# Attention, then two feed-forward layers, on one core: VectorE's next unit waits for GpSimd, and rows of the fixed cycle move

## The chip, the cores and the metric

One NeuronCore of a Trainium2 chip runs the whole program. The metric is device time in microseconds (us) of one execution, the median over repeated runs. Engines are named as the profile names them: PE is TensorE's matmuls and PEld its weight loads, DVE is VectorE, ACT ScalarE, POOL GpSimd, SP SyncE (which here only issues DMAs).

## The reference

```python
scores = (q @ k.T) / sqrt(64)                  # 4 batches x 8 heads, 576 x 576, head size 64
kth    = 32nd largest score of each row
attn   = softmax(scores kept where >= kth)
x = attn @ v                                   # as 2304 tokens x 512
h = x @ w_in;   P = a0 + a1*h + a2*h^2 + a3*h^3      # layer 1, 512 -> 2048 -> 512
Q = 1 + |b0|*|h| + |b1|*h^2;   x = (P / (Q + 1e-6)) @ w_out
h = x @ w2_in;  out = (h * cos(h)) @ w2_out    # layer 2, 512 -> 2048 -> 512
```

Everything is float32. To keep that precision with PE's faster float32 form, each operand is split into a high and a low part, and three products (high x high, low x high, high x low) are summed.

## The kernel before

**Units and groups.** Attention runs in 72 units. A unit is 128 queries by one pair of heads; eight units (4 head pairs by 2 halves) make a block of 256 tokens. In the last eight units, 64 to 71, a unit's queries come from two batches. Each feed-forward layer treats a block in eight groups of 256 hidden columns. The pieces of a unit are generators: `qk` (scores into the PSUM tile `sx`, copied by ACT to `sS`, one copy for each head), `topk` (VectorE folds the scores into pairwise maxima and minima in `e`, two TENSOR_TENSOR rows, finds the 32 largest by MAX8 and MATCH_REPLACE8, then ACT writes the exponentials into `e`, and VectorE masks them by two SCALAR_TENSOR_TENSOR rows), `av` (PE transposes `e` into `pp..a`, `pp..b` and a part of `sx`, ACT copies these to `pt..`, PE multiplies by `v`), and `norm`.

**Layer 1** (line 498 on): `in1` and `in1b` are the two halves of h (24 matmuls); `copy1` makes w = h and r = |w| on ACT, `lin1` q = b1*r + b0 and u = -(a3*w + a2) on ACT, `pol1` q *= r and u *= w on GpSimd, `rec1` 1/Q by Ln and Exp on ACT, `mid1` and `end1` finish the quotient on VectorE and copy its high part to a tile `gg` on ACT, `low1` makes the low part on GpSimd, and `out1` (24 matmuls into `y`) multiplies by w_out. **Layer 2**: `in2`, `in2b`, `copy2` (h to `hs`), `phase2` and `mid2` (argument of the cosine, `rr` and `n`), `sin2` (on every second group, a table load and one Sin for two groups), `mul2`, `high2`, `low2`, and `out2` (12 matmuls of 512 columns into `o`).

**The order.** Early units are placed by a scheduler. From unit U0 = 20 to unit U1 = 72 the order is written out by hand in `unit(i, prev)` (line 843): the wrapper `InOrder` (line 90) chains each engine's instructions in the order in which they are written. A unit works at once on its own maxima, on the masks, transposes and values of unit i-1, on the scores of unit i+2, on layer 1 of group i-9 and i-10, and on layer 2 of groups i-18 to i-21. In a *sine* unit (every second one, the even ones) ACT also computes the Sin.

**VectorE against GpSimd.** `InOrder` makes each GpSimd instruction wait (a semaphore) for the latest VectorE instruction, in written order, that is not a `max` or `match_replace` (`V.shared`, lines 105 to 108). GpSimd's work of a unit thus stands beside VectorE's maxima. Nothing makes VectorE wait for GpSimd at the start of the next unit, other than data.

**Buffers.** `ps_t` has two PSUM buffers, shared in turn by the two transposes, layer 1's h, `norm` and layer 2's h. `gg` has three. Weights' low parts and `w2o` stream through four 512 KB buffers on SP's queue. After unit 71 the functions `free` and `events` order the rest of the feed-forward work.

Of the kernel before, what the change touches and what calls it, by code (L numbers as in the profile page):

```python
# [89 lines left out]
class InOrder(Windowed):  # L90
    def __init__(self, *a, behind=None):
        super().__init__(*a)
        self.last = self.shared = None
        self.behind = behind

    def __getattr__(self, name):
        f = super().__getattr__(name)

        def call(*a, **k):
            r = f(*a, **k)  # L100
            if C0 <= self.piece < C1:
                if self.last is not None:
                    self.tc.add_manual_dep(r.ins, self.last, ORDER, reason="order")
                self.last = r.ins.name
                if self.behind is not None and self.behind.shared is not None:
                    self.tc.add_manual_dep(r.ins, self.behind.shared, WAIT, reason="port")
                if name not in ("max", "match_replace"):
                    self.shared = r.ins.name
            else:
                self.shared = None  # L110
# [5 lines left out]
def body(tc, out, qt, kt, vt, ident_d, w1_d, w1o_d, a_d, b_d, w2_d, w2o_d):  # L116
# [5 lines left out]
    with ExitStack() as ctx:  # L122
# [39 lines left out]
        def store_k(x, b, pr):  # L162
            raw, hi = x[:, 0].bitcast(F32), x[:, 1]
            A.activation(hi, raw, AF.Copy)
            G.tensor_sub(raw, raw, hi.bitcast(F32))
# [3 lines left out]
            for o, i_ in ((d[top, 0], hi[top]), (d[bot, 0], raw[top]), (d[bot, 1], hi[bot]), (d[top, 1], raw[bot])):  # L169
                SP.dma_start(out=o, in_=i_)  # L170

# [332 lines left out]
        def copy1(k, g):  # L504
            h, _ = g1[k, g]
            w, q, r, u = (mo.tile([P, BT * 2], F32, tag="m1" + t, bufs=NU if t == "u" else N1, name=f"{t}{k}_{g}") for t in "wqru")
            A.activation(w, h, AF.Copy)
            A.activation(r, w, AF.Abs)
            g1[k, g] = (q, r, u, w)

        def lin1(k, g):
            q, r, u, w = g1[k, g]
            A.activation(q, r, AF.Identity, scale=b1, bias=b0)
            A.activation(u, w, AF.Identity, scale=na3, bias=na2)

        def pol1(k, g):
            q, r, u, w = g1[k, g]
            E1 = V if k >= DV1 else G
            E1.tensor_mul(q, q, r)
            E1.tensor_mul(u, u, w)  # L520
# [109 lines left out]
        def out2(k, g):  # L630
# [7 lines left out]
            for i, t in steps if g < NG - 1 else sorted(steps, key=lambda x: x[1]):  # L638
                f, ts = 2 * g + i, slice(t * P, (t + 1) * P)
                for l, r in ((gh, 0), (gh, 1), (gl, 0)):  # L640
                    PE.matmul(o[:, t, :], l[:, i, ts], wt[i][:, r], start=(f == 0 and r == 0 and l is gh), stop=(f == NF - 1 and l is gl), skip_group_check=True)
# [92 lines left out]
        nrm, low, held, x2, ob = [], [], [], [], []  # L734
# [74 lines left out]
        def early(u, p):  # L809
            if p == 0:  # L810
                ev(u - UA - 1, mid1)
            if p == 1:
                lows()
                ev(u - UA, in1, in1b, copy1, lin1, pol1, rec1)
# [11 lines left out]
        def events(u, p):  # L826
# [3 lines left out]
            if p == 1:  # L830
# [4 lines left out]
                ev(u - UA, in1, in1b, copy1, lin1, pol1, rec1)  # L835
# [7 lines left out]
        def unit(i, prev):  # L843
            sine = (i - UB - 1) % SINB == SINB - 1
            t = topk(i)
            next(t)
# [3 lines left out]
            next(a)  # L850
            if not sine:
                ev(i - UB - 1, phase2)
            ev(i - UA - 1, mid1, end1)
# [7 lines left out]
            ev(i - UB - 1, mid2)  # L861
            for k in x2:
                x2low(k)
            x2.clear()
            ev(i - UB - 3, low2)
# [9 lines left out]
            if i % 4 == 0:  # L875
                next(nrm[-1])
            high_q(i + 3, True)
            ev(i - UA, in1b, copy1)
# [3 lines left out]
            ev(i - UA, lin1, pol1)  # L882
            ev(i - UB, in2)
            next(nq, None)
            ev(i - UB, in2b)
            for k in ob:
                store(k, 1)
            ob.clear()
            if i + 3 < nu:
# [3 lines left out]
            ev(i - UB - 1, table)  # L893
            for _ in range(4):
                next(t)
            load_v(i)
# [6 lines left out]
            ev(i - UB, copy2)  # L903
            ev(i - UB - 2, high2)
            if not sine or i == U1 - 1:
# [6 lines left out]
            for x, a in held:  # L912
                store_k(x, *a)
            held[:] = [(prep(*a), a) for a in preps.get(i, [])]
# [8 lines left out]
        for u in range(UB + NB * NG + 3):  # L923
            grouped = U0 <= u < U1
            f = free(u, prev) if not grouped and u <= nu else iter(())
            for p in range(5):
# [9 lines left out]
                else:  # L936
                    prev = next(f, prev)
# [42 lines left out]
```

## Time and profile before

| | us |
|---|---|
| median of 3 runs | 1382.33 (1380.45 to 1382.46) |
| the profiled execution, device time | 1381.68 |
| its span, first to last instruction | 1379.7 |
| fixed cycle, roughly 355 to 1190 of the span | 835 |

The profiled execution is a typical run: 0.65 us under the median. Its span is 1.98 us shorter than its device time, so a change of the span is taken as the same change of the time. A row of a list by line gives operation, output<-inputs, shape, count, busy us and mean ns, then the idle time just before these instructions and what ended it. A row of a timeline gives start and duration in us; the bracket is idle time before it and its releaser. Matmuls overlap in the pipe, so their spacing, start to start, is what one costs.

### The profile page before, as it was taken

What the parts mean: (1) busy time and instruction counts of PE and PEld (TensorE: products, weight loads), DVE (VectorE), ACT (ScalarE), POOL (GpSimd) and SP (SyncE); (2) the same over time, 40 slices, a digit from 0 to 9 for tenths busy, and PEclk for the clock granted to TensorE, in tenths of its full rate; (3) what the DMA queues carried; (4) which work ended last, traced back from release to release, by engine and by line L of the source; (5) the groups of instructions that cost most, each with busy time, mean ns of one, the idle gap of its engine ahead of it and who ended that gap; (6) DMA issues with size and microseconds to landing.
All of it is one profiled execution on the core that took longest, in us unless ns stands there. A gap on an engine that the chain in (4) does not pass through costs nothing.

```text
span 1379.7 us, 25048 instructions
## 1 busy us (share of the span) xinstructions
PE 1238.5 (90%) x8944; PEld 1095.0 (79%) x8944; DVE 1183.7 (86%) x2514; ACT 1086.5 (79%) x1869; POOL 585.2 (42%) x483
## 2 busy tenths in 40 slices
PE   7766777666999999999999999999999999999987
PEld 3434555556899898899988998988999899999976
DVE  6999878989999999999999899999999888655532
ACT  7887788775878888888888888888887777877642
POOL 2667545543345544444544454444444343520000
PEclk9677799777999999999999999999999999999999
DMA  8986787873456677666677766666576777677677
GB/s 263 326 279 215 240 244 233 296 256 104 136 188 207 228 238 247 223 197 221 205 230 234 254 207 208 215 219 216 189 238 239 255 264 248 212 229 245 219 236 231
DMA packets 155948, 314.98 MB, mean 228 GB/s; under 512 B 12592, under 2 KB 47536, under 8 KB 155824
## 3 DMA queue, kind: packets, MB, share of 16 engines
q1 hardware_dynamic: 122832, 261.99, 57.5%
q10 hardware_dynamic: 32992, 51.39, 11.6%
q8 instruction: 71, 1.16, 0.3%
q14 instruction: 53, 0.43, 0.1%
HBM read 278.20 MB, written 35.13 MB: 227 GB/s over the span
## 4 chain that ended last, share of the span: by engine, by line
PE 48%; ACT 15%; DVE 14%; DMA 8%; issue 2%; POOL 1%; ACTq 0%; SPq 0%; DVEq 0%; POOLq 0%
PE h L80 18%; PE o L80 11%; PE y L80 10%; PE sx L80 7%; DVE e L80 6%; DVE hd L80 5%; ACT r L80 2%; ACT sS L80 2%; DMA lo<-w1lo 2%; DMA w2o<-w2o 2%; ACT n L80 1%; ACT rr L80 1%; ACT e L80 1%; DVE rr L80 1%; DVE cb L80 1%
## 5 line engine op out<-in xcount | busy, mean ns | idle before, releaser
L80 DVE MAX8 hd<-e 128x8 f32<-128x288 f32 (+1 forms) x576 | 321.2, 597 | 0.0
L80 DVE MATCH_REPLACE8 e<-hd,e 128x288 f32<-128x288 f32 (+1 forms) x432 | 231.2, 542 | 0.0
L80 PE MATMUL y<-gg,w1o 128*128 128x256 f32 x1152 | 217.4, 287 | 7.1 <-POOL gg L80 4.2
L80 POOL TENSOR_TENSOR gg<-rr,gg 128x512 fp32r<-128x512 f32 x56 | 72.8, 1300 | 352.9 <-DVE rr L80 309.6
L80 PE MATMUL o<-w2o,gg 128*128 128x512 f32 x864 | 212.3, 393 | 3.8 <-DMA w2o<-w2o 3.8
L80 PEld LDWEIGHTS y<-gg,w1o 128*128 128x128 f32 x1152 | 183.4, 195 | 9.1 <-POOL gg L80 5.3
L80 PE MATMUL h<-xh,w1hi 128*128 128x256 f32 x576 | 178.6, 310 | 10.3 <-ACT pt41a L80 1.0
L80 PEld LDWEIGHTS o<-w2o,gg 128*128 128x128 f32 x864 | 157.6, 189 | 34.8 <-DMA w2o<-w2o 5.2
L80 PE MATMUL h<-xh,lo 128*128 128x256 f32 x576 | 166.7, 289 | 2.0 <-DMA lo<-w1lo 2.0
L80 PE MATMUL h<-xl,w1hi 128*128 128x256 f32 x576 | 167.3, 291 | 0.0
L80 PE MATMUL h<-x2h,lo 128*128 128x256 f32 x576 | 163.9, 285 | 2.3 <-DMA lo<-w2lo 2.3
L80 PE MATMUL y<-gg,w1ol 128*128 128x256 f32 x576 | 164.6, 286 | 0.0
L80 PE MATMUL h<-x2h,w2hi 128*128 128x256 f32 x576 | 163.5, 284 | 0.5 <-ACT hs L80 0.5
L80 PE MATMUL h<-x2l,w2hi 128*128 128x256 f32 x576 | 163.6, 284 | 0.1
L80 DVE TENSOR_TENSOR e<-sS 128x576 f32<-128x576 f32 x144 | 151.0, 1085 | 6.9 <-ACT sS L80 5.3
L80 PEld LDWEIGHTS h<-xh,w1hi 128*128 128x128 f32 x576 | 114.1, 198 | 29.5 <-issue 5.7
L80 DVE SCALAR_TENSOR_TENSOR e<-sS,hd,e 128x576 f32<-128x576 f32 x144 | 124.2, 889 | 14.2 <-ACT e L80 14.2
L80 POOL TENSOR_TENSOR cb<-cb,raw 128x512 int32<-128x512 int32 x64 | 89.3, 1400 | 103.1 <-DVE cb L80 85.0
L80 ACT ACTIVATE e<-sS,nb 128x576 f32<-128x576 f32 x144 | 105.6, 771 | 22.4 <-DVE hd L80 21.4
L80 PE MATMUL sx<-k,q 128*128 128x288 f32 (+1 forms) x576 | 108.2, 316 | 12.2 <-ACT sS L80 4.9
L80 PEld LDWEIGHTS h<-xh,lo 128*128 128x128 f32 x576 | 113.7, 197 | 2.6 <-DMA lo<-w1lo 2.6
L80 PEld LDWEIGHTS h<-xl,w1hi 128*128 128x128 f32 x576 | 114.1, 198 | 1.5 <-issue 0.5
(1024 smaller groups left out, 3255.8 us busy)
## 6 DMA issues: line engine op xcount, KB each, us to landing
w2o<-w2o SPq DMA_DIRECT2D x144, 512.0 KB, 4.4
lo<-w1lo SPq DMA_DIRECT2D x72, 512.0 KB, 4.2
w1ol<-w1ol SPq DMA_DIRECT2D x72, 512.0 KB, 4.8
lo<-w2lo SPq DMA_DIRECT2D x72, 512.0 KB, 4.1
k<-kdr ACTq DMA_DIRECT2D x44, 576.0 KB, 4.2
raw<-w SPq DMA_DIRECT2D x32, 512.0 KB, 5.1
v<-vt ACTq DMA_DIRECT2D x48, 320.0 KB, 4.4
qr<-qt ACTq DMA_DIRECT2D x72, 128.0 KB, 3.4
```

The lines of the kernel that those rows point to most:

```text
L80: r = f(*a, **k)
```

## The change

1. `V.ahead = G.last`: from unit 21 on, the first VectorE instruction of a unit (the first of the two TENSOR_TENSOR rows into `e`) waits for the last GpSimd instruction of the unit before.
2. In units that are not sine units, `mid2` moves behind the first maxima (max, replace, max) and is *quiet*: GpSimd doesn't wait for it.
3. `copy1` takes over `lin1` and writes w, u, r, q; `pol1` multiplies u by w first, then q by r.
4. The second head's scores stand behind all 24 matmuls of layer 2's input, no longer between its halves; their copy to `sS` stands behind the exponentials on ACT.
5. `out2` issues six matmuls, and the other six (`out2b`) behind the next transposes.
6. Phases move: `phase2`, `high2`, `copy2`, the splitting of k for the later batches (`split_k`) and one step of `norm` stand elsewhere in the unit, most of them split between sine and other units.

```diff
@@ InOrder.__getattr__
+                if self.ahead is not None:
+                    self.tc.add_manual_dep(r.ins, self.ahead, WAIT, reason="port")
+                    self.ahead = None
-                if name not in ("max", "match_replace"):
+                if name not in ("max", "match_replace") and not self.quiet:
                     self.shared = r.ins.name
@@ copy1, lin1, pol1
             A.activation(w, h, AF.Copy)
+            A.activation(u, w, AF.Identity, scale=na3, bias=na2)
             A.activation(r, w, AF.Abs)
+            A.activation(q, r, AF.Identity, scale=b1, bias=b0)
...
+            E1.tensor_mul(u, u, w)
             E1.tensor_mul(q, q, r)
-            E1.tensor_mul(u, u, w)
@@ out2
+            part(steps[:2])
+            if U0 <= PE.piece // 5 < U1:
+                rest2.append((part, steps[2:]))
+            else:
+                part(steps[2:])
@@ unit
+            if i > U0:
+                V.ahead = G.last
             next(t)
             next(prev)
             next(prev)
             a = av(i - 1)
             next(a)
+            out2b()
+            ev(i - UA - 1, mid1, end1)
             if not sine:
+                ev(i - UB - 3, high2)
                 ev(i - UB - 1, phase2)
-            ev(i - UA - 1, mid1, end1)
+                for x, a_ in held:
+                    split.append(split_k(x, *a_))
+                    next(split[-1])
+                held.clear()
...
-            ev(i - UB - 1, mid2)
             for k in x2:
                 x2low(k)
             x2.clear()
+            if not sine:
+                next(t)
+                V.quiet = True
+            ev(i - UB - 1, mid2)
+            V.quiet = False
...
-            if i % 4 == 0:
+            if i % 8 == 0 or i % 8 == 5:
                 next(nrm[-1])
+            for x in split:
+                next(x, None)
+            split.clear()
             high_q(i + 3, True)
-            ev(i - UA, in1b, copy1)
+            ev(i - UA, in1b, copy1, pol1)
             load_q(i + 4)
             nq = qk(i + 2) if i + 2 < nu else iter(())
             next(nq, None)
-            ev(i - UA, lin1, pol1)
-            ev(i - UB, in2)
-            next(nq, None)
-            ev(i - UB, in2b)
+            ev(i - UB, in2, in2b)
...
+            ev(i - UB - 1, table)
+            if not sine:
+                ev(i - UB, copy2)
+                ev(i - UB - 2, high2)
+            for _ in range(4 if sine else 3):
+                next(t)
+            next(nq, None)
+            load_v(i)
...
             ev(i - UA - 1, out1)
             ev(i - UB - 3, out2)
-            ev(i - UB - 1, table)
-            for _ in range(4):
-                next(t)
-            load_v(i)
+            if sine:
+                ev(i - UB, copy2)
             ev(i - UA, rec1)
...
-            ev(i - UB, copy2)
-            ev(i - UB - 2, high2)
-            if not sine or i == U1 - 1:
+            if not sine:
                 ev(i - UB, phase2)
...
-            for x, a in held:
-                store_k(x, *a)
-            held[:] = [(prep(*a), a) for a in preps.get(i, [])]
+            held.extend((prep(*x), x) for x in preps.get(i, []))
```

Three places as the instructions stand in the program. First TensorE between units 40 and 42: `o2` is layer 2's output, `pp41` the transposes of unit 41, `h0_4_1` layer 1's input. Before:

```order
L80 MATMUL o2_6769<-w2o2_8_7453,gg2_4_7408 128x512 x6
L80 MATMUL o2_6769<-w2o2_9_7455,gg2_4_7408 128x512 x6
L80 MATMUL pp41a_7630<-ident_98,e41_7412 128x128 x4
L80 MATMUL pp41b_7637<-ident_98,e41_7412 128x128 x4
L80 MATMUL sx_91<-ident_98,e41_7412 128x128
L80 MATMUL h0_4_1_7664<-xh4_7402,w1hi_116 128x256
```

Of the change:

```order
L80 MATMUL o2_6790<-w2o2_8_7460,gg2_4_7441 128x512 x6
L80 MATMUL pp41a_7624<-ident_98,e41_7404 128x128 x4
L80 MATMUL pp41b_7631<-ident_98,e41_7404 128x128 x4
L80 MATMUL sx_91<-ident_98,e41_7404 128x128
L80 MATMUL o2_6790<-w2o2_9_7462,gg2_4_7441 128x512 x6
L80 MATMUL h0_4_1_7664<-xh4_7398,w1hi_116 128x256
```

Six matmuls went from ahead of the transposes to behind them. Second, ScalarE in unit 41, from the copy of layer 1's h on (`w4_0` to `q4_0`), with the two score copies `sS43` and the exponentials `e41`. Before:

```order
L80 ACTIVATE w4_0_7495<-h0_4_0_7457 128x512
L80 ACTIVATE r4_0_7497<-w4_0_7495 128x512
L80 DMA qr45_7501<-qt 128x2x128
L80 ACTIVATE sS43_7503<-sx_91 128x576
L80 ACTIVATE q4_0_7496<-r4_0_7497,babs_105 128x512
L80 ACTIVATE u4_0_7498<-w4_0_7495,nega_107 128x512
L80 ACTIVATE sS43_7503<-sx_91 128x576
L80 DMA k44_2_7545<-kdr_90 128x1152
L80 ACTIVATE nb_41_7414<-hd_41_7413 128x2
L80 ACTIVATE e41_7412<-sS41_7089,nb_41_7414 128x576 x2
```

Of the change:

```order
L80 ACTIVATE w4_0_7507<-h0_4_0_7464 128x512
L80 ACTIVATE u4_0_7510<-w4_0_7507,nega_107 128x512
L80 ACTIVATE r4_0_7509<-w4_0_7507 128x512
L80 ACTIVATE q4_0_7508<-r4_0_7509,babs_105 128x512
L80 DMA qr45_7517<-qt 128x2x128
L80 ACTIVATE sS43_7519<-sx_91 128x576
L80 ACTIVATE hs2_7_7552<-h1_2_7_7527 128x512
L80 ACTIVATE gg2_5_7554<-rr2_4_7031 128x512
L80 ACTIVATE nb_41_7406<-hd_41_7405 128x2
L80 ACTIVATE e41_7404<-sS41_7099,nb_41_7406 128x576 x2
L80 ACTIVATE sS43_7519<-sx_91 128x576
L80 DMA k44_2_7572<-kdr_90 128x1152
```

The first score copy now stands behind u, r and q, the second behind the exponentials. Third, VectorE in unit 41 around the row of the phase (`rr2_6`), and at the start of unit 42, with the semaphores that each row waits for. Before:

```order
L80 TENSOR_TENSOR q43_7276<-qr43_7087,q43_7276 128x256 [waits DMAHW4_49]
L80 SCALAR_TENSOR_TENSOR rr2_6_7437<-n2_6_7438,rr2_6_7437 128x512 [waits Activation_49]
L80 MAX hd_41_7413<-e41_7412 128x8 x2
...
L80 TENSOR_TENSOR e42_7623<-sS42_7298 128x2x288 [waits PE_49]
L80 TENSOR_TENSOR e42_7623<-sS42_7298 128x2x288
```

Of the change:

```order
L80 TENSOR_TENSOR q43_7276<-qr43_7097,q43_7276 128x256 [waits DMAHW4_49]
L80 MAX hd_41_7405<-e41_7404 128x8 x2
L80 MATCH_REPLACE e41_7404<-hd_41_7405,e41_7404 128x288 [waits DVE_49] x2
L80 MAX hd_41_7405<-e41_7404 128x8 [waits DVE_49] x2
L80 SCALAR_TENSOR_TENSOR rr2_6_7443<-n2_6_7444,rr2_6_7443 128x512 [waits Activation_49]
...
L80 TENSOR_TENSOR e42_7617<-sS42_7302 128x2x288 [waits PE_49,Pool_49]
L80 TENSOR_TENSOR e42_7617<-sS42_7302 128x2x288
```

The phase's row went behind six rows of maxima, and the first row of unit 42 has a wait for GpSimd more.

## Rows read from the trace of the kernel before

**Rows 1.** Page: busy us, share of the span and instructions of each engine.

```profile
PE 1238.5 (90%) x8944; PEld 1095.0 (79%) x8944; DVE 1183.7 (86%) x2514; ACT 1086.5 (79%) x1869; POOL 585.2 (42%) x483
```

**Rows 2.** One stretch, the cycle: length, busy of PE, PEld, DVE, ACT, POOL, granted clock, DMA.

```profile
355.00:1190.00 835.00, 815.31 (x6435) 749.12 (x6435) 771.38 (x1711) 700.95 (x1187) 388.01 (x331) 1.00 0.67 222
```

**Rows 3.** List by line, PEld alone, 355 to 1190 us; idle time is the last part.

```profile
L80 PEld LDWEIGHTS h<-xh,w1hi 128*128 128x128 f32 x416 | 78.8, 190 | 27.7 <-issue 5.7 <-ACT pt41a L80 1.2 <-ACT pt25a L80 1.2
L80 PEld LDWEIGHTS sx<-k,q 128*128 128x128 f32 x472 | 65.7, 182 | 14.8 <-ACT sS L80 14.3
```

**Rows 4.** Waits of PEld, 355 to 1190 us: total us, times, longest.

```profile
PEld h L80 <- issue: 5.7, 33, 0.2
PEld h L80 <- DMA lo<-w1lo: 2.6, 3, 1.0
```

**Rows 5.** Timeline of PEld: transposes of units 22, 41, 42, 63, unit 41's two waits.

```profile
392.37 0.59 PEld L80 LDWEIGHTS pp21a<-ident,e 128*128 128x128 f32 x4
...
692.97 0.59 PEld L80 LDWEIGHTS pp40a<-ident,e 128*128 128x128 f32 x4
...
694.48 0.19 PEld L80 LDWEIGHTS h<-xh,w1hi 128*128 128x128 f32 x1 [0.38 <-ACT pt40a L80]
...
701.25 0.56 PEld L80 LDWEIGHTS sx<-k,q 128*128 128x128 f32 x4 [0.34 <-ACT sS L80]
...
708.71 0.58 PEld L80 LDWEIGHTS pp41a<-ident,e 128*128 128x128 f32 x4
...
1041.55 0.58 PEld L80 LDWEIGHTS pp62a<-ident,e 128*128 128x128 f32 x4
```

**Rows 6.** Timeline of PE in unit 41: output 2, transposes, scores, both halves of input 2.

```profile
690.44 2.92 PE L80 MATMUL o<-w2o,gg 128*128 128x512 f32 x12
693.20 0.60 PE L80 MATMUL pp40a<-ident,e 128*128 128x128 f32 x4
...
698.98 0.70 PE L80 MATMUL sx<-k,q 128*128 128x288 f32 x4
699.52 0.28 PE L80 MATMUL h<-x2h,w2hi 128*128 128x256 f32 x1
...
701.88 0.28 PE L80 MATMUL h<-x2h,w2hi 128*128 128x256 f32 x1
```

**Rows 7.** Timeline of ACT, units 40 and 41, from h's copy on.

```profile
684.17 0.63 ACT L80 ACTIVATE r<-w 128x512 f32<-128x512 f32 x1
684.79 0.65 ACT L80 ACTIVATE sS<-sx 128x576 f32<-128x576 f32 x1
685.34 0.81 ACT L80 ACTIVATE q<-r,babs 128x512 f32<-128x512 f32 x1
686.04 0.80 ACT L80 ACTIVATE u<-w,nega 128x512 f32<-128x512 f32 x1
...
687.40 1.28 ACT L80 ACT_TABLE_LOAD   x1
...
688.93 0.78 ACT L80 ACTIVATE e<-sS,nb 128x576 f32<-128x576 f32 x1
...
699.24 0.60 ACT L80 ACTIVATE w<-h 128x512 f32<-128x512 f32 x1 [1.41 <-PE h L80]
```

**Rows 8.** Timeline of POOL at the end of unit 40.

```profile
686.22 1.30 POOL L80 TENSOR_TENSOR q<-q,r 128x512 f32<-128x512 f32 x1 [0.74 <-ACT q L80]
687.48 1.81 POOL L80 TENSOR_TENSOR u<-u,w 128x512 f32<-128x512 f32 x1
```

**Rows 9.** Timeline of DVE, units 40 to 42.

```profile
672.69 1.41 DVE L80 TENSOR_TENSOR e<-sS 128x576 f32<-128x576 f32 x2
...
686.62 3.28 DVE L80 TENSOR_TENSOR e<-sS 128x576 f32<-128x576 f32 x2
...
690.56 0.81 DVE L80 SCALAR_TENSOR_TENSOR e<-sS,hd,e 128x576 f32<-128x576 f32 x1
...
696.48 0.69 DVE L80 SCALAR_TENSOR_TENSOR rr<-n,rr 128x512 f32<-128x512 f32 x1 [0.91 <-ACT n L80]
```

More of the change, by code (lines that the diff above doesn't have):

```diff
@@ L92, in __init__ @@
         super().__init__(*a)
-        self.last = self.shared = None
+        self.last = self.shared = self.ahead = None
+        self.quiet = False
         self.behind = behind
@@ L160, in load_k0, with split_k @@
             return x
-        def store_k(x, b, pr):
+        def split_k(x, b, pr):
             raw, hi = x[:, 0].bitcast(F32), x[:, 1]
             A.activation(hi, raw, AF.Copy)
+            yield
             G.tensor_sub(raw, raw, hi.bitcast(F32))
@@ L170, in store_k @@
                 SP.dma_start(out=o, in_=i_)
+        def store_k(*a):
+            for _ in split_k(*a):
+                pass
         def prep(b, pr):
@@ L507, in copy1 @@
             A.activation(w, h, AF.Copy)
+            A.activation(u, w, AF.Identity, scale=na3, bias=na2)
             A.activation(r, w, AF.Abs)
+            A.activation(q, r, AF.Identity, scale=b1, bias=b0)
             g1[k, g] = (q, r, u, w)
[L511 to L514, printed above, removed]
         def pol1(k, g):
@@ L637, in out2, with part, out2b @@
             steps = [(i, t) for i in range(2) for t in range(2)]
[L638 to L641, printed above, removed]
+            if g == NG - 1:
+                steps.sort(key=lambda x: x[1])
+            def part(steps):
+                for i, t in steps:
+                    f, ts = 2 * g + i, slice(t * P, (t + 1) * P)
+                    for l, r in ((gh, 0), (gh, 1), (gl, 0)):
+                        PE.matmul(o[:, t, :], l[:, i, ts], wt[i][:, r], start=(f == 0 and r == 0 and l is gh), stop=(f == NF - 1 and l is gl), skip_group_check=True)
+            part(steps[:2])
[3 more added lines that the diff above has]
+                part(steps[2:])
+        rest2 = []
+        def out2b():
+            for part, steps in rest2:
+                part(steps)
+            rest2.clear()
         def store(k, t):
@@ L732, in body @@
                 preps.setdefault(16 * b - PL + pr if b == 1 else 16 * b - PL + 2 + 2 * pr, []).append((b, pr))
-        nrm, low, held, x2, ob = [], [], [], [], []
+        nrm, low, held, split, x2, ob = [], [], [], [], [], []
         def free(i, prev):
@@ L813, in early @@
                 lows()
-                ev(u - UA, in1, in1b, copy1, lin1, pol1, rec1)
+                ev(u - UA, in1, in1b, copy1, pol1, rec1)
             if p == 2:
@@ L834, in events @@
                 ev(u - UB - 2, mul2, high2)
-                ev(u - UA, in1, in1b, copy1, lin1, pol1, rec1)
+                ev(u - UA, in1, in1b, copy1, pol1, rec1)
             if p == 2:
@@ L936, in body @@
                 else:
+                    out2b()
                     prev = next(f, prev)
```

## The prediction

> **What bounds the kernel now.** I read the busy shares first, then the stretch, then who waits for whom on the two fullest engines, then one pair of units line by line. Over the whole span PE and VectorE are both near 90% [rows 1], which decides nothing. The change acts on the fixed cycle, 835 us of 1379.7; there the clock is granted in full and VectorE is busy 771.38/835 = 92%, PE's weight loads 749.12/835 = 90% [rows 2]. The waits decide which of them paces. PE has three waits in the cycle, and none is for VectorE: 27.7 us before layer 1's first weights, of which 5.7 is issue and 22.0 is ACT's copy of the transposes (0.38 in unit 41), 14.8 before the scores, nearly all of it the second head waiting for the first head's copy (0.34 in unit 41), and 2.6 for a DMA [rows 3 to 5]. All else on PE stands back to back: twelve matmuls of layer 2's output take 693.20 - 690.44 = 2.76 us, 0.23 each [rows 6].
>
> VectorE, for all its busy time, is early. In unit 41 its last mask ends at 690.56 + 0.81 = 691.37 and the transposes that need it start at 692.97, 1.60 later [rows 5, 9]. It is also held back: the two TENSOR_TENSOR rows take 3.28 us where they take 1.41 undisturbed, as GpSimd's last two products run from 686.22 to 689.29 [rows 8, 9], and it waits 0.91 for the phase `n`. GpSimd's products wait for ACT's q, which waits for PE's h. So PE paces a unit of (1041.55 - 392.37)/41 = 15.83 us [rows 5], and VectorE's stretched rows fill time that it has. I therefore price the change by PE's waits, and then ask whether anything else becomes longer than PE's unit.
>
> **Part 1, six output matmuls behind the transposes.** They are 6 x 0.23 = 1.38 us of work that needs only `gg` and `w2o`, both there since the unit before. The wait for ACT's copy is 0.38, so it is covered in a common unit. After a unit that ends a block, ACT also copies `x2h` ahead of it and the wait was up to 1.2 [rows 3]; I leave 0.4 of it in five such units, 2.0 in all, rounded down to 1.5 because the cover is 1.38. Gain: 22.0 - 1.5 = 20.5 us. A new cost may be one more change of weights from transposes to output to input; the nearest row is the "issue" wait of 0.17 (5.7 us in 33) [rows 4], so between 0 and 52 x 0.17 = 8.8 us. I take 0, since twelve output matmuls run into the transposes at 0.23 spacing without it.
>
> The price is lead: transposes come 1.38 earlier in PE's order, against a lead of 1.60. That would leave 0.2 if VectorE stayed where it is; parts 3 and 4 say where it goes.
>
> **Part 2, scores around layer 2's input.** One head's scores take 699.52 - 698.98 = 0.54, and 701.88 - 699.52 = 2.36 holds 12 matmuls, the second scores and the wait of 0.34, so a matmul is 0.12 [rows 5, 6]. Cover for the first head's copy grows from 12 matmuls to 24, from 1.44 to 2.87. But ACT now does u, r and q ahead of that copy. From the start of the first scores (698.98) [rows 6]: w starts at 0.26 [rows 7], and ACT's spacings are 0.63 for a copy, 0.70 for u and for q (685.34 to 686.04), 0.62 for r [rows 7], so the score copy starts at 0.26 + 0.63 + 0.70 + 0.62 + 0.70 = 2.91 and ends at 3.56, with 0.06 to PE 3.62. PE is ready at 0.54 + 2.87 = 3.41. **The wait stays, at about 0.2 instead of 0.33.** Gain 44 x 0.1 = 4 us, between 0 and all of the 14.8.
>
> **Part 3, VectorE waits for GpSimd's last product.** With T = 0 at a unit's transposes, PE's new order reaches the first scores at 698.98 - 693.20 - 0.38 + 1.38 = 6.78. ACT's w starts at 7.04, u is ready at 8.37, q at 9.69. GpSimd needs 1.30 for each [rows 8]: u until 9.7, q until 11.05. Before, w began near 683.5 (0.63 before r) and u ended at 689.29, 5.8 later; now both are done 4.0 after w. VectorE starts its unit at 11.1, the pair of rows takes 1.33, the masks 0.74 and 0.81. In a sine unit ACT loads its table before the exponentials: score copy until 10.34, table until 11.6, exponentials two of 0.74 from 11.9 (688.93 - 687.40 = 1.53 after the load's start) to 13.4 [rows 7], so the second mask ends at 14.2. PE's unit is then 15.74 (708.71 - 692.97) [rows 5] - 0.38 - 0.1 = 15.25. **VectorE is done 1.05 us before the next transposes; the wait falls on its own slack and costs 0.** Its own undisturbed work is 13.93 (672.69 to 686.62) [rows 9], below 15.25. Queued behind the waiting row are its second half, both masks and the transposes; nobody else is held earlier. What shows is a new wait of VectorE, up to 1.6 us in sine units, whose maxima end first.
>
> A TENSOR_TENSOR stretched to let GpSimd finish and a row that waits for it end alike, by the 3.28 row. The Trainium skill, "SBUF — State Buffer", section "Who interferes with whom", says the same more strictly: a VectorE instruction with two SBUF inputs and a reading GpSimd instruction exclude each other for whole instructions. By that rule the semaphore is no gain of its own, and where two products are left it forbids the row that VectorE now slips between them; my sum has 0 for it either way, and the loss is in the third rival.
>
> **Part 4, the quiet phase row and the moved steps.** In the other units the 0.91 wait for `n` goes behind 2.3 us of maxima, and GpSimd starts earlier by 0.69 + 0.91. The moved row can meet a GpSimd product and lose up to 1.30 or gain the 0.91: it lies on VectorE, with a second of slack, 0. `split_k` puts 1.6 us of GpSimd into such units, eight times; there q ends some 0.8 later, still inside the 1.05. Four SP stores come with it, a unit earlier than before, ahead of loads that are needed half a unit later: 0. The second half of `w2o` frees its buffer some 1 us later in the cycle; its successor is needed a unit later: 0, with the 2.6 of DMA waits as the bound both ways.
>
> **Outside the cycle** only the order u, r, q of ACT and GpSimd changes, in eleven units before and nine after, and the scheduler shuffles rows around it. I take 0; if each unit won or lost half an ACT spacing of 0.7 us, it would be 7 us either way.
>
> **Sum:** -20.5 - 4 = -24.5 on 1381.68, that is 1357.2; the profiled run is 0.65 under the median, so **1357.5 us**.
>
> **The rivals.**
>
> *VectorE paces, or all PE waits go.* For it: VectorE's 92% is above the weight loads' 90% [rows 2], and shortening its held rows is what the title says. The Trainium skill, "Perfetto Trace Analysis", section "Identifying the Most-Contended Engine", takes the engine with the highest occupancy and, for PE, the weight loads' share: by that rule VectorE. Against: its lead of 1.60. Then the gain is not parts 1 and 2 but ends only when PE has no wait left: 22.0 + 14.8 + 2.6 = 39.4, **1343 us**.
>
> *The scores stay behind ACT.* ACT has four copies ahead of the score copy, so each 0.1 us by which it reaches w late now costs PE 0.1. For it: four copies in place of two stand between h and that score copy. Against: ACT sat idle 1.41 before w in unit 41 [rows 7], and h comes a microsecond later after the transposes now. If 0.25 us in each of 52 units comes back, 13 us are lost: **1370 us**.
>
> *Slower: GpSimd's last product comes after VectorE needs it.* GpSimd's products have taken 1.81 instead of 1.30 when they met VectorE [rows 8], and the quiet row takes the port from it once. If two of them stretch (1.0) and the quiet row delays it 0.69, q ends 1.7 later than worked out, VectorE's masks come 1.7 - 1.05 = 0.65 after PE wants its transposes, and PE waits that in each unit: 52 x 0.65 = 34 us against 24.5 gained, **1392 us**. It decides from about 1.5 us of lateness; below 1.05 it costs nothing. Against: maxima have one input, and GpSimd's window lies among them.
>
> *The change does nothing.* The PE waits that go return before the transposes (0.2 us of lead is all that part 1 leaves if VectorE doesn't move up): within 2.7 us of **1382**.
>
> **How the numbers follow.** A difference of 0.2%, 2.8 us, is about what a measurement of this kernel can tell. Chances: forecast 0.58, all waits gone 0.10, scores behind ACT 0.15, slower 0.10, nothing 0.07. Faster by over 0.2% are the first three, 0.83; same 0.07; slower 0.10. The range goes from 1343 (every PE wait gone) to 1376: the forecast with the 8.8 of weight changes and 7 of the early units against it is 1373, and the second rival with half of either is 1376 to 1378. The slower and the idle case, 0.17, are left out.
>
> **What would show it.** Right: no wait of layer 1's first weights for `pt` in common units; a wait of the second scores near 0.2; a wait of VectorE's first row for GpSimd in sine units and TENSOR_TENSOR pairs at 1.4 throughout; a unit near 15.3. Wrong: transposes that wait for VectorE's `e` (the slower rival or the idle one), score waits over 0.4 (the second), or PE without any score wait (the first).

## The result, and the profile after

| | before | after |
|---|---|---|
| median | 1382.39 us, 4 runs, 1380.45 to 1385.25 | 1364.78 us, 4 runs, 1361.69 to 1367.21 |
| profiled execution, span | 1381.68, 1379.7 | 1366.73, 1364.9 |

The ratio is 0.987, interval [0.984, 0.99]: 17.6 us faster by the medians, where 24.9 were forecast. All of it is won in the cycle, and some is lost ahead of it and behind it. I cut both spans at the transposes of units 20, 22 and 71 (`pp19a`, `pp21a`, `pp70a` in the list of PEld, which starts the index one lower):

| stretch | before | after | difference |
|---|---|---|---|
| start to unit 20's transposes | 356.46 | 362.50 | +6.0 |
| to unit 22's | 35.91 | 35.57 | -0.3 |
| to unit 71's ("the cycle" below) | 786.17 | 763.85 | -22.3 |
| to the end | 201.16 | 202.98 | +1.8 |

The four add up to the -14.8 us between the spans.

The busy time of the engines in the cycle, before (columns as in [rows 2]):

```profile
392.37:1178.54 786.17, 769.83 (x6045) 707.11 (x6044) 727.15 (x1616) 662.43 (x1120) 364.34 (x312) 1.00 0.69 226
```

and after, where the first line is the page's for the whole span:

```profile
PE 1236.2 (91%) x8944; PEld 1098.8 (80%) x8944; DVE 1172.0 (86%) x2514; ACT 1092.2 (80%) x1869; POOL 585.1 (43%) x483
...
398.07:1161.92 763.85, 758.95 (x6042) 704.40 (x6043) 715.94 (x1616) 666.69 (x1120) 364.38 (x312) 1.00 0.71 232
```

VectorE's busy time fell by 11.2 us and the weight loads' by 2.7. The first is a net figure: the pairs of TENSOR_TENSOR rows, which no longer stretch beside GpSimd, take 32.5 us less, and the rows of the phase 22.1 more (their lines stand below). It does not say where the 22.3 come from. That is in PE's waits, the rows of [rows 3, 4], now by line (355 to 1190 us, as there) and then by releaser (the cycle alone):

```profile
L80 PEld LDWEIGHTS h<-xh,w1hi 128*128 128x128 f32 x424 | 81.2, 191 | 12.3 <-issue 5.7 <-ACT pt20a L80 1.2 <-ACT pt71b L80 0.7
L80 PEld LDWEIGHTS sx<-k,q 128*128 128x128 f32 x472 | 66.0, 182 | 12.1 <-ACT sS L80 10.9 <-ACT xs L80 1.2
...
PEld sx L80 <- ACT sS L80: 9.5, 40, 0.2
PEld h L80 <- issue: 5.5, 32, 0.2
PEld h L80 <- DVE xl L80: 3.9, 5, 0.8
PEld pp45a L80 <- PE o L80: 0.9, 1, 0.9
```

The 27.7 us before layer 1's first weights are 12.3, the 14.8 before the scores 12.1. Added up from the single waits (those over 0.15 us) in the cycle: for the transposes' copies 20.8 before and 2.5 now, for the first head's score copy 12.4 and 9.5, for a weight DMA 2.6 and none, for `hs` and a load of v 0.7 and 0.6 and none. Waits for `xl` grew from 0.4 to 3.9 (in the first unit of a block of layer 1), and transposes now wait 2.6 for `e`, in units 30 and 46 and at the start of the cycle. The list puts 1.8 of those down to the output matmuls, `o`, which is PE itself; PE stands there because VectorE's mask is late. Together -19.0; of the remaining 3.3, 2.7 are the shorter weight loads and 0.6 waits under 0.15 us. The line of the score copy before, beside the 9.5 above:

```profile
PEld sx L80 <- ACT sS L80: 12.4, 40, 0.4
```

PEld in unit 41, to be read beside [rows 5]:

```profile
691.66 0.59 PEld L80 LDWEIGHTS pp40a<-ident,e 128*128 128x128 f32 x4
...
694.99 0.19 PEld L80 LDWEIGHTS h<-xl,w1hi 128*128 128x128 f32 x1 [0.76 <-DVE xl L80]
...
702.88 0.56 PEld L80 LDWEIGHTS sx<-k,q 128*128 128x128 f32 x4 [0.24 <-ACT sS L80]
...
706.26 1.24 PEld L80 LDWEIGHTS o<-w2o,gg 128*128 128x128 f32 x6
707.54 0.58 PEld L80 LDWEIGHTS pp41a<-ident,e 128*128 128x128 f32 x4
...
708.64 1.23 PEld L80 LDWEIGHTS o<-w2o,gg 128*128 128x128 f32 x6
```

Two pieces of output stand around the transposes, and no row waits for `pt` in a common unit. The unit is 15.19 us where nothing special happens and 15.9 in the first unit of a block; on the average of units 22 to 62 it is 15.46, before 15.82. VectorE in the same place:

```profile
687.80 1.43 DVE L80 TENSOR_TENSOR e<-sS 128x576 f32<-128x576 f32 x2 [0.97 <-POOL q L80]
...
690.03 0.81 DVE L80 SCALAR_TENSOR_TENSOR e<-sS,hd,e 128x576 f32<-128x576 f32 x1
...
692.25 0.69 DVE L80 SCALAR_TENSOR_TENSOR q<-q,r 128x512 f32<-128x512 f32 x1 [0.73 <-ACT r L80]
...
698.10 1.02 DVE L80 SCALAR_TENSOR_TENSOR rr<-n,rr 128x512 f32<-128x512 f32 x1
...
704.56 1.43 DVE L80 TENSOR_TENSOR e<-sS 128x576 f32<-128x576 f32 x2 [0.48 <-POOL q L80]
...
706.64 0.81 DVE L80 SCALAR_TENSOR_TENSOR e<-sS,hd,e 128x576 f32<-128x576 f32 x1
```

The pair of rows that took 3.28 [rows 9] takes 1.43, behind a wait for GpSimd of 0.97 or 0.48. The masks end at 690.84 and 707.45, 0.82 us and 0.09 us ahead of the first weight load of their transposes (691.66 and 707.54); by the same count it was 1.60 before. Over the cycle this lead depends on the kind of unit (I name a unit by the `e` that is masked and transposed, these two are `e40` and `e41`). In the sine units up to `e60` it is 0.5 to 0.8. In the others it is about 0.4 in the commonest kind (`e23`, `e35`, `e39`, `e51`, `e55`, `e59`). In eight (the odd ones of `e25` to `e31` and `e41` to `e47`) GpSimd also splits k, the row `kraw` below; there it goes from 0.14 down to -0.6, which is a second mask that ends after the transposes have begun. The rest lie between -0.1 and 0.7. In VectorE's rows a wait for `r` of 0.73 is new. Over the cycle, the first two lines before, the others after:

```profile
L80 DVE TENSOR_TENSOR e<-sS 128x576 f32<-128x576 f32 x98 | 102.2, 1082 | 0.0
L80 DVE SCALAR_TENSOR_TENSOR rr<-n,rr 128x512 f32<-128x512 f32 x49 | 33.2, 678 | 42.8 <-ACT n L80 42.8
...
L80 DVE TENSOR_TENSOR e<-sS 128x576 f32<-128x576 f32 x98 | 69.7, 753 | 24.5 <-POOL q L80 24.4
L80 DVE SCALAR_TENSOR_TENSOR rr<-n,rr 128x512 f32<-128x512 f32 x49 | 55.3, 1128 | 0.0
L80 DVE SCALAR_TENSOR_TENSOR q<-q,r 128x512 f32<-128x512 f32 x49 | 33.8, 690 | 18.1 <-ACT r L80 18.1
```

The wait for `r` is 18.1 us, of which the prediction says nothing. The phase's row waited 42.8 us for `n` before, 24 times and up to 2.4, and waits no longer: the 0.91 of [rows 9], from which the prediction worked, was one of the short ones. GpSimd in unit 41:

```profile
696.04 1.29 POOL L80 TENSOR_TENSOR gg<-rr,gg 128x512 fp32r<-128x512 f32 x1 [8.28 <-DVE q L80]
697.28 1.29 POOL L80 TENSOR_TENSOR gg<-u,gg 128x512 fp32r<-128x512 f32 x1
698.51 1.76 POOL L80 TENSOR_TENSOR rr<-rr,hs 128x512 f32<-128x512 f32 x1
700.24 1.44 POOL L80 TENSOR_TENSOR kraw<-kraw 128x576 f32<-128x576 f32 x1
...
703.24 1.28 POOL L80 TENSOR_TENSOR q<-q,r 128x512 f32<-128x512 f32 x1
```

The quiet phase row (698.10) meets two of these and is stretched to 1.02, and GpSimd's own `rr` to 1.76. The last product ends at 704.52, 12.6 us after the transposes.

### The profile page after: what moved, and what is told of

The parts are those of the page before. It is cut to its first block, busy times and chain, and to the rows that moved or that the text cites. A ratio compares the mean times of both kernels' runs of the same rounds, so it can differ in the third digit from the quotient of the medians.

```text
span 1364.9 us, 25054 instructions
## 1 busy us (share of the span) xinstructions
PE 1236.2 (91%) x8944; PEld 1098.8 (80%) x8944; DVE 1172.0 (86%) x2514; ACT 1092.2 (80%) x1869; POOL 585.1 (43%) x483
## 4 chain that ended last, share of the span: by engine, by line
PE 59%; DVE 18%; ACT 10%; DMA 6%; POOL 3%; issue 3%; ACTq 0%; SPq 0%; POOLq 0%; DVEq 0%
PE h L80 24%; PE o L80 11%; PE y L80 10%; PE sx L80 10%; DVE e L80 8%; DVE hd L80 4%; DVE cb L80 2%; DVE u L80 2%; ACT r L80 2%; DMA w2lo<-cb 1%; ACT e L80 1%; DMA w2o<-w2o 1%; ACT sS L80 1%; ACT cb L80 1%; DMA raw<-w2o 1%
## 5 line engine op out<-in xcount | busy, mean ns | idle before, releaser
L80 PE MATMUL y<-gg,w1o 128*128 128x256 f32 x1152 | 227.7, 296 | 23.6 <-ACT gg L80 11.0
L80 PE MATMUL o<-w2o,gg 128*128 128x512 f32 x864 | 225.3, 399 | 3.6 <-DMA w2o<-w2o 3.0
L80 PEld LDWEIGHTS y<-gg,w1o 128*128 128x128 f32 x1152 | 191.8, 203 | 28.7 <-ACT gg L80 14.1
L80 PEld LDWEIGHTS o<-w2o,gg 128*128 128x128 f32 x864 | 153.8, 189 | 31.9 <-DMA w2o<-w2o 2.5
L80 PE MATMUL h<-xh,w1hi 128*128 128x256 f32 x576 | 173.4, 301 | 1.5 <-ACT pt20a L80 1.0
L80 PE MATMUL y<-gg,w1ol 128*128 128x256 f32 x576 | 169.2, 294 | 0.0
L80 DVE TENSOR_TENSOR e<-sS 128x576 f32<-128x576 f32 x144 | 116.5, 848 | 41.3 <-POOL q L80 30.3
L80 PEld LDWEIGHTS y<-gg,w1ol 128*128 128x128 f32 x576 | 117.2, 203 | 0.4 <-issue 0.3
```

## The experiments

Twelve kernels ran. Times are medians; "cycle", "ahead" (of unit 20's transposes) and "rest" are the stretches above, from the profiled run.

**1. The scheduler's early rows.** Outside the cycle `copy1`, `lin1` and `pol1` get their old order back; ScalarE's and GpSimd's rows of the early units are then those of the kernel before.

```diff
-            A.activation(u, w, AF.Identity, scale=na3, bias=na2)
+            if C0 <= A.piece < C1:
+                A.activation(u, w, AF.Identity, scale=na3, bias=na2)
...
+            if not C0 <= A.piece < C1:
+                A.activation(u, w, AF.Identity, scale=na3, bias=na2)
```

> The change, but outside the fixed cycle ScalarE keeps w, r, q, u and GpSimd q, u, so that the units ahead of the cycle stand as before, row for row. Theory (the changed order let the scheduler place units 16 to 19 worse, which cost 6 us ahead of the cycle): unit 20's transposes (of e19) come near 356.5 instead of 362.5, the cycle stays at 764 us from the transposes of e21 to those of e70, and the time is 1358 to 1360. Rival (the 6 us are how the clock was granted in that execution): unit 20 comes anywhere between 356 and 363 and the time is within 2 us of 1364.8.

1359.6 us, ratio 0.9821 [0.9787, 0.9854]: ahead 359.75, cycle 763.50, rest 200.28. The time is the theory's; the 359.75 lies between the two, and the interval overlaps that of the change, so this run alone doesn't decide (experiment 12 comes back to it). The cycle is that of the change; what differs stands ahead of it and behind it. This kernel is the base of the later ones.

**2 and 4. The split of the output, taken out and alone.** Experiment 2 is the change with all twelve output matmuls ahead of the transposes; experiment 4 is the kernel before with nothing but the split (`out2b` behind the next transposes).

```diff
-            if U0 <= PE.piece // 5 < U1:
+            if False:
                 rest2.append((part, steps[2:]))
```

> The change with all twelve output matmuls ahead of the transposes again. Theory (TensorE paces the cycle and the gain is its wait for the copies of the transposes): the wait of layer 1's first weights for pt is back at 0.38 a unit, the cycle (transposes of e21 to e70: 786.2 before, 763.9 with the change) is 780 to 784, the time 1381 to 1385. Rival (the gain came from VectorE, which no longer meets GpSimd): the cycle stays below 770.

> The kernel before with one part of the change alone, six output matmuls behind the transposes. Theory (part 1 is worth 0.38 a unit, and the lead of 1.4 to 1.6 us covers the 1.38 by which the transposes move up): the cycle falls from 786 to 766 to 772, the time to 1363 to 1368. Rival (VectorE, unmoved, makes the transposes wait, and the other parts are needed): the cycle is 775 to 786, with transposes that wait for VectorE's e by 0.2 or more in most units.

Experiment 2: 1376.87 us, 0.9943 [0.9922, 0.9964], cycle 777.11. So the split is worth 13.3 us in the change (777.11 - 763.85), and all the rest of the change 9.1 (786.17 - 777.11). The waits for `pt` are back at 18.8, those for the score copy are 9.0. The cycle lies between the ranges of theory and rival: the `pt` waits came back, as the theory said, but 9.1 us stay. Experiment 4: 1373.53 us, 0.9911 [0.9881, 0.9942], cycle 773.44, 12.7 shorter, again between the two ranges. Its PEld, by line and by releaser:

```profile
L80 PEld LDWEIGHTS h<-xh,w1hi 128*128 128x128 f32 x392 | 74.4, 190 | 10.6 <-issue 5.5 <-ACT pt41a L80 0.8 <-ACT pt25a L80 0.7
L80 PEld LDWEIGHTS sx<-k,q 128*128 128x128 f32 x448 | 62.2, 181 | 14.1 <-ACT sS L80 12.6 <-POOL gg L80 1.4
...
PEld pp64b L80 <- ACT hs L80: 2.4, 1, 2.4
PEld pp48b L80 <- ACT hs L80: 1.0, 1, 1.0
```

The `pt` waits go here too, but six times the second transposes wait for `hs`, 7.5 us in all: they share the two PSUM buffers with layer 2's h, and 1.4 us earlier they catch up with its copy. The change has that copy earlier in the unit, and the wait is gone. It comes instead as 3.9 for `xl` and 2.6 for `e`.

**3. No wait for GpSimd.** The two lines with `V.ahead` are left out.

> The change without VectorE's wait for GpSimd's last product; all else as in the change. Theory (the wait falls on VectorE's own slack, and a stretched row ends when a waiting one would): the cycle stays at 762 to 766, the pair of TENSOR_TENSOR rows is again 2 to 3 us in sine units. Rival (the semaphore is what frees VectorE and with it TensorE): the cycle is 772 or more. A third way, that the wait costs something: below 761.

1362.98 us, 0.9845 [0.9812, 0.9878]; cycle 763.48 against 763.85. The semaphore is worth nothing in the cycle, as the theory said. Without it VectorE is busy 17.2 us longer, in the same time: its rows stretch where they would have waited.

```profile
394.97:1158.45 763.48, 758.74 (x6043) 704.15 (x6044) 733.09 (x1618) 666.44 (x1120) 366.17 (x312) 1.00 0.69 233
```

At the entry, from unit 20's transposes to unit 22's, this profile took 32.8 against 35.6. There VectorE waits for a GpSimd that is still behind:

```profile
379.53 1.43 DVE L80 TENSOR_TENSOR e<-sS 128x576 f32<-128x576 f32 x2 [5.54 <-POOL q L80]
```

(that row is the changed kernel's). In experiment 1, with the same semaphore, the wait is 1.25 and the entry 34.7, so what it costs there is not shown.

**5 and 6. More cover for the scores.** Experiment 5 is experiment 1 with the second head's scores behind layer 1's output too; 6 adds the reciprocal (and the sine units' `copy2`) ahead of the second score copy on ScalarE, and `V.ahead` from unit 22.

```diff
             for _ in range(4 if sine else 3):
                 next(t)
+            ev(i - UA - 1, out1)
+            ev(i - UA, rec1)                 # experiment 6 alone
             next(nq, None)
             load_v(i)
```

> e1 with the second head's scores one step later still, behind layer 1's 24 output matmuls; ScalarE's order is untouched. The wait for the first head's copy (0.24 us a unit, 10 us in e1's cycle) has 2.9 us more cover. Theory (TensorE still paces, and this wait is its largest): the wait goes and the cycle falls from 763.5 to 753 to 758, the time to 1350 to 1355. Rival (VectorE's lead before the transposes, 0.1 to 0.8 us, is used up and VectorE now paces): the score wait goes, transposes wait for VectorE's e instead, the cycle stays above 760.

> e5, and ScalarE does the two reciprocal steps (Ln, Exp) ahead of the second score copy, so that VectorE no longer waits 0.7 us for r at the start of every second unit; also VectorE's wait for GpSimd begins at unit 22, not 21 (there it cost 5.5 us of VectorE once). Theory (VectorE's lead is what limits e5): the waits of VectorE for r (19 us) go, its lead before the transposes grows by 0.3 to 0.7 us, the cycle falls to 750 to 755 and is at least 2 us below e5's; the time 1345 to 1352. Rival (TensorE is bound by its own work): the cycle is within 1 us of e5's and only the entry gains.

Experiment 5: 1390.75 us, 1.0049 [1.0029, 1.0069], slower than the kernel before; neither theory had that. ScalarE takes its rows in written order, and in unit 41 of experiment 5 its timeline is

```profile
704.71 0.65 ACT L80 ACTIVATE sS<-sx 128x576 f32<-128x576 f32 x1 [0.67 <-PE sx L80]
...
705.26 0.72 ACT L80 ACTIVATE r<-q,qc 128x512 f32<-128x512 f32 x1
...
707.92 1.06 ACT L80 ACTIVATE x2h<-y 128x512 fp32r<-128x512 f32 x2
708.88 0.60 ACT L80 ACTIVATE pt41a<-pp41a 128x512 f32<-128x512 f32 x1
```

while PE waits for the end of that queue:

```profile
709.53 0.19 PEld L80 LDWEIGHTS h<-xh,w1hi 128*128 128x128 f32 x1 [1.52 <-ACT pt41a L80]
```

The score copy now waits for PE, and behind it stand the reciprocal, the phase and the transposes' copies. The score waits went, and 22.9 us of `pt` waits came back, with VectorE's wait for `r` at 51.5. The cycle is 31.2 us longer than experiment 1's, 10.1 of it from unit 22's transposes to unit 62's (628.4 against 618.27) and 19.0 in units 64 to 71 (132.4 against 113.4), which this queue explains only in part.

Experiment 6: 1370.59 us, 0.9899 [0.9868, 0.993], cycle 770.32, far from the theory's 750 to 755. From unit 22's transposes to unit 62's it took 605.25 us, and the commonest unit 14.89; there the rows moved ahead on ScalarE are worth 23.1. But units 64 to 71 took 131.3, as in experiment 5. There each unit has queries of two batches and needs two new k tiles, and two are all there are. Waits of 1056 to 1170 us in experiment 6:

```profile
PEld sx L80 <- issue: 8.4, 4, 2.4
...
PE sx L80 <- DMA k<-kdr: 5.6, 3, 2.2
```

Loads of k and v are issued on ScalarE's queue behind the second score copy; PEld also waits 3.1 for loads of v there. The order that gives the scores more cover in the common units seems to make these loads late in the last eight, which experiments 10 and 11 test.

**7. The phase row ahead of the maxima again**, not quiet, on experiment 1.

```diff
+            ev(i - UB - 1, mid2)
             if not sine:
                 next(t)
-                V.quiet = True
-            ev(i - UB - 1, mid2)
-            V.quiet = False
```

> e1 with the phase row back ahead of the maxima in units that are not sine units, and GpSimd waiting for it again. Theory as predicted (the row lies on VectorE's slack): the cycle stays at 763 to 767. Rival (VectorE has only 0.1 to 0.7 us of lead there; it waits for n again and GpSimd starts 1.5 us later): the transposes wait for e in these units, the cycle is 770 or more.

1394.11 us, 1.0066 [1.0045, 1.0088], cycle 783.41: 19.9 us of the cycle's 22.3 are lost. VectorE, GpSimd and PE in it, by line and by releaser:

```profile
L80 DVE SCALAR_TENSOR_TENSOR rr<-n,rr 128x512 f32<-128x512 f32 x49 | 33.2, 677 | 46.8 <-ACT n L80 46.8
...
POOL gg L80 <- DVE rr L80: 391.1, 46, 10.1
...
PEld pp29a L80 <- issue: 2.9, 1, 2.9
...
PE pp29a L80 <- DVE e L80: 2.5, 1, 2.5
```

The rival was right. In the changed kernel the phase's row waits 0.0 for `n`. Here it waits 46.8 in 24 units, hardly more than the 42.8 before; but the transposes come earlier now, and measured from them the row starts later, 5.26 us after their first weight load in most of these units, where it was 3.51 before. Two high copies stand ahead of the phase on ScalarE now, layer 1's and layer 2's, 1.05 us together in unit 41 of the changed kernel:

```profile
694.37 0.63 ACT L80 ACTIVATE gg<-u 128x512 fp32r<-128x512 f32 x1
694.90 0.62 ACT L80 ACTIVATE gg<-rr 128x512 fp32r<-128x512 f32 x1
695.42 0.71 ACT L80 ACTIVATE rr<-hs,quarter 128x512 f32<-128x512 f32 x1
```

All of GpSimd's products queue behind the row, the last one ends later, VectorE's next unit begins later, and the transposes wait for `e`, 21.5 us in the cycle against 2.6. The experiment puts back the row's place and GpSimd's wait for it together, so it doesn't tell which of the two costs how much.

**8. q first in the cycle too** (on experiment 1: ScalarE w, r, q, u and GpSimd q, u everywhere).

> e1 with the old order of ScalarE's copies (w, r, q, u) and of GpSimd's products (q, u) in the cycle too; the scores still stand around all of layer 2's input. Theory (u first lets GpSimd start 1.3 us earlier, which is VectorE's lead now): GpSimd's last product ends 0.7 to 1.3 us later, VectorE's wait for it grows by as much, the transposes wait in units with little lead, and the cycle is 770 to 785. Rival (there is slack for it): the cycle stays below 767.

1367.5 us, 0.9872 [0.9846, 0.9897]; cycle 765.77, rest 204.46. The rival was right: the order is worth 2.3 us in the cycle, in score waits (11.9 against 9.5); the 4.2 in the rest, where u and q stand in the same order in both kernels, are not explained.

**9. The reciprocal early, scores where the change has them.**

```diff
+            ev(i - UA, rec1)
+            if sine:
+                ev(i - UB, copy2)
             next(nq, None)
```

> The kernel of e1_early_order_old (1359.6 us) with layer 1's reciprocal (and the sine units' copy of layer 2's h) ahead of the second head's score copy on ScalarE, and VectorE's wait for GpSimd from unit 22 on instead of 21; the scores stay where the change has them. It takes away VectorE's wait for r, 18.9 us in 29 times in the cycle, and the wait of 5.5 at the entry. Theory A (PE paces, and VectorE's wait for r fell on its slack): the cycle from the transposes of unit 22 to those of unit 71 stays at 763.5, and only the entry between the transposes of units 20 and 22 gets shorter by up to 2.8, about 1357 us. Theory B (VectorE's lateness still costs PE something, seen in the transposes that wait 3.5 us for e in units with a table load): the cycle loses those 3.5 us as well and perhaps the 3.9 of the waits for xl, 1350 to 1354 us. Theory C (the second score copy, now behind Ln and Exp, holds sx from the next values): new waits of PE for the copy, slower than 1359.6.

1364.95 us, 0.9859 [0.9846, 0.9873]. Units 22 to 62 gain 4.5 (613.76): VectorE no longer waits for `r`, `xl` comes in time, and the units with 15.9 are at 15.19. Units 64 to 71 lose 4.4 (117.75), with waits for loads of k again, and the rest 3.3, of which 2.3 are a wait for a load of v; the cycle is 764.08, no gain. Theory B was right for the common units alone, and C's longer time came, but not by a wait for the score copy (9.8 against 9.5).

**10 and 11. Each order where it fits.** Experiment 10 is 6 with the scores where the change has them from unit 61 on; 11 puts the reciprocal back there as well.

```diff
+            if i < 61:
+                ev(i - UA - 1, out1)
+                rest()                       # reciprocal, copy2
             next(nq, None)
             load_v(i)
...
             ev(i - UB - 3, out2)
+            if i >= 61:
+                rest()
```

> The kernel of e6_and_reciprocal_early (1370.6 us; its units 22 to 62 took 605.3 against 618.3 in e1, but its units 64 to 71 took 131.3 against 113.4), with the second head's scores behind the output of layer 1 only up to unit 60 and where the change has them from unit 61 on. Theory A (two k tiles are all there are, and from unit 64 on each unit needs two new ones, so a load of k can start only when the scores of the unit before are done; scores that stand 3 us later then make PE wait for the load): units 22 to 62 stay near 605, units 64 to 71 return to about 113.5, 1345 to 1349 us. Theory B (the late units lose time to ScalarE's order of reciprocal and score copy, not to the place of the scores): units 64 to 71 stay above 125, about 1362 us or more.

> The kernel of e10_scores_late_until_unit_61 (1357.7 us; units 64 to 71 took 117.6, the rest behind them 204.2) with the reciprocal, too, where the change has it from unit 61 on, so that ScalarE issues the loads of k and v without Ln and Exp ahead of them. Theory A (what is left of the loss in the late units is these loads, issued by ScalarE behind the second score copy): units 64 to 71 return to 113.4 and the rest to about 201, so 6 to 8 us faster than e10 in the cycle and behind it, about 1350 us. Theory B (the loss there comes with the units ahead, which run faster than DMAs bring k and v): it stays near 117.6, and the time near 1357.

Experiment 10: 1357.72 us, 0.9805 [0.9778, 0.9833]; units 22 to 62 605.52, units 64 to 71 117.56. Theory A for the place, less the 4 us that experiment 9 had lost in the same place; the time missed its 1345 to 1349. Experiment 11: **1348.65 us, 0.973 [0.9707, 0.9754]**, with 113.34 in units 64 to 71, and no wait for a load of k there: theory A again. It is faster than both kernels, 36.6 us under the kernel before of the same session. Its cycle:

```profile
389.86:1142.15 752.29, 749.01 (x6044) 702.25 (x6044) 715.96 (x1616) 663.84 (x1120) 364.61 (x312) 1.00 0.71 236
...
L80 PEld LDWEIGHTS sx<-k,q 128*128 128x128 f32 x448 | 62.8, 182 | 0.2 <-ACT sS L80 0.2
...
PEld h L80 <- DVE xl L80: 1.1, 5, 0.3
```

VectorE's busy time is that of the changed kernel to 0.1 us; the 11.6 us are in the main PE's score waits, 9.5 to 0.2, and the waits for `xl`, 3.9 to 1.1.

**12. The change's early order on experiment 11.**

> The kernel of e11 with the order w, u, r, q of ScalarE and u, q of GpSimd everywhere, as the change has it, and no longer in the cycle alone; so the scheduler shuffles the rows of the early units as in the changed kernel. Theory A (the shuffle costs, as the first profiles said: the transposes of unit 20 at 362.2 to 363.3 in three of them against 356.5 to 359.8 in the first with the old order): 3 to 5 us slower than e11, nearly all of it ahead of those transposes. Theory B (the early part differs by the granted clock of its first 350 us from run to run, and the later profiles with the old order, up to 364.5, are the evidence): the same as e11 within 2 us.

1351.5 us, 0.9766 [0.974, 0.9791], 2.9 more than experiment 11, with intervals that overlap a little; cycle 751.53 and rest 201.07 are nearly the same. Ahead of unit 20 the ten profiles with the old rows took 356.2 to 364.5, 358.8 on average, the four with the change's rows 362.2 to 366.2, 363.5 on average. PE has 1345 or 1346 matmuls in this stretch with the change's rows, 1322 with the old. But the early part also differs from run to run with the clock, here in experiment 11 and then 12 (the column behind POOL is the granted clock, a mix of its 2.4 and 1.2 GHz):

```profile
60.00:120.00 60.00, 39.83 (x174) 23.52 (x173) 59.91 (x125) 48.68 (x98) 38.31 (x29) 0.76 0.89 293
```

```profile
60.00:120.00 60.00, 43.98 (x164) 25.86 (x163) 57.76 (x116) 45.66 (x91) 37.98 (x28) 0.64 0.86 280
```

0.76 was seen in five of the ten with the old rows and in none of the four with the new; but 0.64 was also seen twice with the old. At like clocks the two sets are closer: at 0.71 to 0.72, 358.4 to 359.8 (experiments 1, 4 and 8) against 362.2 and 362.5; at 0.64, 361.3 and 364.5 against 363.3 and 366.2. So some 2 to 3 us go with the scheduler's rows, from few profiles and with ranges that overlap at 0.64. Why, stays open.

## Why the prediction was right, and where its steps were not

**What bounds the kernel: right.** PE paces, and VectorE's 92% was not the limit: the cycle got 22.3 us shorter, and PE's waits account for 19.0 of it. The rival by which VectorE paces promised 39.4. The rule of the Trainium skill, "Perfetto Trace Analysis", "Identifying the Most-Contended Engine", points at VectorE in the changed kernel too (715.94 of 763.85 against 704.40 of the weight loads), and experiment 11 then took 11.6 us out with VectorE's busy time unchanged, while experiment 3 added 17.2 to it and the cycle stayed. The trace does not bear the rule out here.

**Part 1, -20.5: right in the wait, too large in the sum.** The `pt` waits fell by 18.3; of the rest, 2.5 lie in six units of 0.3 to 0.5, near the 0.4 that was left in five. The step that failed is "the price is lead", priced at nothing: the split was worth 13.3 in the change and 12.7 alone (experiments 2 and 4). Transposes that come 1.4 us earlier run into whatever made them possible: `hs` in experiment 4, VectorE's `e` and `xl` in the change. No wait from a change of weights was seen, as assumed: the "issue" waits are 5.5 in the cycle of both kernels.

**Part 2, -4: right.** The score copy was to start 2.91 us after the first scores and to free PE at 3.62; in unit 41 it starts at 702.19 - 699.27 = 2.92, and the second scores at 3.61. These are the first scores on PE and the copy on ScalarE:

```profile
699.27 0.70 PE L80 MATMUL sx<-k,q 128*128 128x288 f32 x4
...
702.19 0.63 ACT L80 ACTIVATE sS<-sx 128x576 f32<-128x576 f32 x1
```

The wait is 0.24 where 0.2 was worked out; 2.9 us in the cycle. No experiment took this part out alone.

**Part 3, 0: right.** The semaphore moved nothing in the cycle (experiment 3), the order u first 2.3. The lead of 1.05 that was worked out for a sine unit, counted to the first matmul of the transposes, is to the hundredth what `e40` shows (690.84 to 691.89), which is chance in the last digit. What the Trainium skill, "SBUF — State Buffer", "Who interferes with whom", says agrees with the trace here too, to about 0.15 us: the phase's row of 1.02 (698.10 to 699.12) fits a row of 0.69 that starts when GpSimd's product ends near 698.5, and GpSimd's 1.76 (698.51 to 700.27) fits one of 1.30 that starts when the phase's row ends.

**Part 4, 0: the sum stood, its reasons did not.** The quiet row was costed as one that shifts on a second of slack. It is what makes the rest of the change possible: without it 19.9 us of the cycle go (experiment 7). I had taken the 0.91 of one unit for the wait for `n`; in most of the 24 units it was about 2. I had also not followed that two copies, moved ahead of the phase on ScalarE, make `n` later after the transposes. And the slack of the other units is not over 1: it is about 0.4 in the commonest kind and 0.09 in `e41`. I had left out VectorE's 18.1 us of waiting for `r`. Its reciprocal stands behind the second score copy, which part 2 had moved; I followed that copy as far as PE and not to what is queued behind it. Where experiment 9 takes this wait away, the lead of the commonest kind is 1.0 to 1.2, but that of `e41` is -0.14: what `split_k` adds on GpSimd was to stay inside the 1.05 and does not. Here one sign of being wrong showed, transposes that wait for `e`, for 2.6 us of the cycle; two of the three units are of this kind (`e29`, `e45`).

**Part 4, the DMAs: within the bound.** The 2.6 of waits for a weight load are gone, an end of the bound that was given, not the 0 that was taken.

**Outside the cycle, 0 within 7: at its edge.** In the profiles it cost 6.0 ahead and 1.8 behind, less 0.3 at the entry, 7.5 in all; some 2 to 3 of it go with the early rows (experiment 12).

**The sum.** In the cycle 22.3 of the 24.5, by other amounts: part 1 gave 13, the rest 9, of which the experiments price the quiet row, the semaphore and the order of u, but not the place of the scores and the other moved steps. That the sum came so near is in part luck: new waits took 6.1 back (3.5 for `xl`, 2.6 for `e`), and the weight DMA, `hs`, the load of v and shorter weight loads, which the sum had at nothing, gave 6.6. What the forecast lacks by the medians, 7.3, is the early part for the most. The upper end of the range is not worked out right: the second rival's 1370 with half of the 8.8 or half of the 7 is 1374, and 1378 only with half of both.

## What to carry to other kernels

Price a change of order by the waits of the engine that paces, taken over all units and not from one pair, and then follow each moved row in both directions on its own queue: what it waits for now, and everything written behind it, down to DMA issues (in experiments 5 and 6 the last units lost 19 and 18 us, more than the cover was worth). Where a matmul is moved to hide a wait, count the lead of what comes earlier for it, unit kind by unit kind, since the least of them decides. An order that is best in common units can be worst where buffers turn over faster; let it depend on the unit, as experiment 11 does.

## What was not expected

Rows that a scheduler places far ahead of the edited region moved with the edit, and cost some 2 to 3 us. Scores moved back to take 10 us of waits away made the kernel 31 us slower (1359.6 to 1390.75): 10 in the common units, where a score copy of 0.65 us on ScalarE waited for PE with others queued behind it, and 19 in the last eight, where loads also came late. And in the early 350 us, the same rows took from 356.2 to 364.5 us from run to run, at granted clocks of 0.64 to 0.76 between 60 and 120 us: differences under 8 us in one profile's span say nothing unless the stretch is cut out.
